# A retention layer and a low-rank mixer on one core: the joint chunk's halves loaded with their own batch, q^T evacuated by two engines, first outputs through two bank pairs, zero matmuls in TensorE's gaps

## The chip, the cores and the metric

The kernel runs on one core of a Trainium2 chip. The metric is the device time of one execution in microseconds (us). The kernel before took 341.96 us as the median of six runs (340.9 to 342.36).

## The reference

q, k and v are (8 batches, 8 heads, 576 positions, 64). The first half is retention: scores times a decay by distance, times v. Its output, with the heads side by side, is x of the second half, a mixer along the sequence with a low rank (32) and a two-layer perceptron.

```python
scores = scale * np.matmul(q, k.transpose(0, 1, 3, 2))
gamma = 1.0 - 2.0 ** (-5.0 - np.arange(H))
Dmat = np.where(rel >= 0, gamma[:, None, None] ** rel[None, :, :], 0.0)
attn = np.matmul(scores * Dmat[None, :, :, :], v)          # (8, 8, 576, 64)
x = attn.transpose(0, 2, 1, 3).reshape(8, 576, 512)
h = x.transpose(0, 2, 1) @ U @ V                           # U (576, 32), V (32, 576)
u = x + h.transpose(0, 2, 1)
out = u + np.maximum(u @ w_ch1, 0.0) @ w_ch2               # (512, 2048), (2048, 512)
```

Inputs and output are float32.

## The kernel before

**Tiling.** Two batches make a pair p: 1152 positions, 9 chunks of 128. Chunks 0 to 3 are of the first batch, 5 to 8 of the second; chunk 4, XC in the code, is the joint chunk: 64 last positions of the first batch (partitions 0 to 63) and 64 first ones of the second (64 to 127). The factor gamma^(m-n) is split: q is scaled by gamma^m (`qscale`), v by gamma^-n (`vscale`), so that a chunk needs only a triangular mask.

**Steps of a chunk.** `load` (L363) issues the loads of k, q, v from SP and the casts to bf16 (ACT, POOL or DVE; the v cast applies the scale, L307). q and k are transposed by TensorE (`t_pe`, L439), in later pairs by a DMA (`t_dma`, L429). `SC` (L502) makes the scores of the chunk with itself in the bank pair `ps_sc` (or, with `apart`, in two of the three banks `ps_big`) and DVE masks them into `ret` (L533). `ST` (L465) adds k^T v to the state S in the bank `ps_s`, and ACT copies it out: `s_sb` (L495), or `sx` (L491) for the last state of the first batch. `RV` (L563) makes ret v plus q S of the chunk before in `ps_o`, and it is copied out as x: in pair 0 as two halves, ACT (L598) and DVE (L600), in later pairs by one DVE instruction (L606). `MA` (L621) makes a = U^T x of a batch, copied out by ACT (`a_sb`, L641). `MH` (L647) adds the mixer's part on DVE, giving u (L670).

**The perceptron** goes over 9 groups of 4 chunks (`mlp`, L731). Y1 is 16 units of 4 matmuls of 128x512 (`uT` by `w1`), each copied out with a relu by ACT (L752). Y2 is 16 units of 4 (4 row tiles by 4 blocks of `w2`), after which DVE adds u (L776) and POOL issues the store (L782). For groups 0 and 1, u^T is built by TensorE (`build`, L689): x^T by matmuls with the identity, plus V^T a, copied out as `uT` (L720, L722).

**The start.** q of batch 0, chunks 0 to 3, comes as one block of 1 MB, four positions beside each other in a partition (`load_q4`, L309); `t_q4` (L329) transposes it and undoes the order while evacuating it (L357 on ACT, L359 on DVE, 512 columns each). Batch 1 has the same with chunks 5 to 8. The loads of pair 0 and of the weights are chained one behind the other in `line` (L957 to 963). The weights come in 16 pieces of 512 KB through six slots, each cast by POOL (L846, L864). POOL also casts V and copies it (`VV`, L816, L824, L826) and U (`UU`, L820).

**The order of the work.** Each step is an Op with an engine, an assumed duration, dependences and a priority, and the planner (`Plan.run`, L52) lists them in the order in which it would run them. The instructions are emitted in that order, so each engine's queue is fixed by the plan, and an instruction that waits holds up all behind it on its engine. Pair 0 is listed by `batch0` (L873) and `batch1` (L899), the others by `front`. Group 0's perceptron is interleaved with batch 1, group g's with batch g+1.

## Time and profile before

| what | value |
|---|---|
| median of six runs | 341.96 us |
| the profiled execution, its own time | 341.8 us |
| its span, first to last instruction | 339.7 us |
| PE busy, mean granted clock | 320.0 us, 0.984 |
| first Y1 matmul of group 0, first Y2 | 30.14, 44.85 us |
| first Y1 matmul of group 1 | 72.68 us |
| last matmul ends | 334.7 us |

All times are from the span's start. PE is TensorE's matmuls, PEld its weight loads, DVE, ACT and POOL are Vector, Scalar and GpSimd engines, SP the one that issues most DMAs (its queue is SPq). A line of the timeline gives start, length, engine, line of the kernel, operation, tiles, shapes and count, and in brackets how long the engine was idle before it and who ended that. A line of the waits gives who waited for whom, the sum in us, how often and the longest. A line of the chain gives start, length and what the work that ended last was doing then. Most matmuls are emitted by one helper (L278), so their tiles tell them apart.

### The profile page before, as it was taken

The page shows a single profiled execution, that of the slowest core. Times are in us where ns is not written, and L with a number is a line of the kernel's source. Part 1 is how long each engine was busy: PE and PEld are TensorE (multiplying, and loading weights), DVE is VectorE, ACT ScalarE, POOL GpSimd, SP SyncE. Part 2 cuts the span into 40 slices and gives each one's busy share as a digit, 9 for nine tenths or more (in the row PEclk, how much of TensorE's full clock was granted, in tenths as well). Part 3 has the DMA queues.
Part 4 walks back from the last instruction along what each step waited for, and adds up shares of the span by engine and source line. Part 5 has one row for each costly group of instructions (what it writes and reads, how often), then busy time and mean ns, then how long its engine had stood idle before and what let it go on. Part 6 is the DMA issues. An engine that isn't in the chain of part 4 may idle for free.

```text
span 339.7 us, 5955 instructions
## 1 busy us (share of the span) xinstructions
PE 320.0 (94%) x2412; PEld 159.1 (47%) x2412; DVE 152.2 (45%) x227; ACT 132.6 (39%) x234; POOL 86.4 (25%) x116
## 2 busy tenths in 40 slices
PE   1689998999999999999999999999999999999993
PEld 0464444556545444554455445445544444444441
DVE  3563128887656646573377429632533020010011
ACT  3455645268601660165214521363135207405600
POOL 5686764142212313131132004200010010010010
PEclk9859999999999999999999999999999999999999
DMA  8999999999999999999999999603110320011011
GB/s 207 203 304 390 385 241 259 203 236 204 230 206 209 229 200 216 214 219 205 199 184 239 204 219 208 158 15 48 62 64 15 71 85 31 0 68 57 0 64 63
DMA packets 153387, 56.19 MB, mean 165 GB/s; under 512 B 144752, under 2 KB 146800, under 8 KB 153360
## 3 DMA queue, kind: packets, MB, share of 16 engines
q1 hardware_dynamic: 150640, 46.90, 68.2%
q0 software_dynamic: 2720, 8.92, 7.8%
q8 instruction: 19, 0.31, 0.4%
q14 instruction: 8, 0.07, 0.1%
HBM read 36.92 MB, written 9.44 MB: 136 GB/s over the span
## 4 chain that ended last, share of the span: by engine, by line
PE 88%; DVE 4%; SPq 3%; POOL 2%; DMA 1%; issue 1%; ACT 1%; POOLq 0%; DVEq 0%
PE ps_big_t L278 73%; PE ps_o L278 6%; PE ps_s L278 5%; PE ps_sc L278 3%; SPq L385 2%; DMA st_st<-in_q_dram 1%; DVE ret_t L533 1%; DVE qkv_t L403 1%; DVE qkv_t L307 1%; PE ps_big_t L452 1%; POOL VV L816 1%; POOL qkv_t L307 1%; DVE o_sb L776 0%; ACT qkT_t L357 0%; DVE x_t L600 0%
## 5 line engine op out<-in xcount | busy, mean ns | idle before, releaser
L278 PE MATMUL ps_big_t<-uT_t,w_sb 128*128 128x512 bf16 x576 | 133.7, 379 | 0.0
L278 PE MATMUL ps_big_t<-w_sb,y_t 128*128 128x512 bf16 x576 | 133.1, 379 | 0.0
L752 ACT ACTIVATE y_t<-ps_big_t 128x512 bf16<-128x512 f32 x144 | 86.0, 597 | 93.7 <-PE ps_big_t L278 93.5
L278 PEld LDWEIGHTS <-w_sb 128*128 128x128 bf16 x576 | 53.9, 98 | 62.4 <-issue 1.9
L278 PEld LDWEIGHTS <-y_t 128*128 128x128 bf16 x576 | 53.8, 98 | 61.5 <-issue 1.1
L776 DVE TENSOR_TENSOR o_sb<-ps_big_t,u_t 128x512 f32<-128x512 f32 x36 | 24.8, 689 | 90.3 <-PE ps_big_t L278 90.3
L782 POOL DMA_DIRECT2D out_dram<-o_sb x34 | 19.4, 570 | 173.1 <-DVE o_sb L776 166.7
L307 POOL TENSOR_TENSOR qkv_t<-st_st,vscale 128x512 bf16<-128x512 f32 x32 | 33.4, 1046 | 55.6 <-DMA st_st<-in_v_dram 44.4
L533 DVE TENSOR_TENSOR ret_t<-ps_sc,tri 128x1024 bf16<-128x1024 f32 x30 | 36.6, 1219 | 19.5 <-PE ps_sc L278 17.8
L495 ACT ACTIVATE s_sb<-ps_s 128x512 bf16<-128x512 f32 x28 | 16.7, 596 | 60.3 <-PE ps_s L278 60.3
L606 DVE TENSOR_TENSOR x_t<-ps_o,qscale 128x512 bf16<-128x512 f32 x27 | 18.6, 689 | 16.8 <-PE ps_o L278 16.7
L670 DVE TENSOR_TENSOR u_t<-ps_s,x_t 128x512 bf16<-128x512 f32 x20 | 13.8, 691 | 22.1 <-PE ps_s L278 22.0
L403 DVE CAST qkv_t<-st_st 128x512 bf16<-128x512 f32 x27 | 19.2, 712 | 4.1 <-DMA st_st<-in_k_dram 4.1
L278 PEld LDWEIGHTS <-qkT_t 64*128 64x128 bf16 (+2 forms) x576 | 14.7, 99 | 13.5 <-issue 7.2
L278 PEld LDWEIGHTS <-ret_t 128*128 128x128 bf16 (+1 forms) x320 | 13.4, 103 | 9.4 <-DVE ret_t L533 1.6
L278 PE MATMUL ps_sc<-qkT_t 64*128 64x128 bf16 (+1 forms) x304 | 13.5, 219 | 4.0 <-ACT qkT_t L459 2.1
L278 PE MATMUL ps_o<-qkv_t,ret_t 128*128 128x64 bf16 (+1 forms) x320 | 15.3, 198 | 0.9 <-DVE x_t L600 0.5
L278 PE MATMUL ps_s<-qkv_t 128*128 128x128 bf16 (+1 forms) x128 | 13.3, 230 | 0.3 <-POOL qkv_t L307 0.3
L459 ACT ACTIVATE qkT_t<-ps_big_t 128x512 bf16<-128x512 bf16 x20 | 11.4, 598 | 3.3 <-PE ps_big_t L452 3.2
L403 DVE CAST qkv_t<-q_st 128x512 bf16<-128x512 f32 x27 | 11.9, 440 | 1.3 <-DMA q_st<-in_q_dram 1.2
L278 PEld LDWEIGHTS <-qkv_t 128*128 128x128 bf16 (+1 forms) x128 | 9.3, 102 | 5.9 <-issue 1.9
L670 DVE TENSOR_TENSOR u_t<-ps_o,x_t 128x512 bf16<-128x512 f32 x16 | 11.0, 685 | 1.7 <-PE ps_o L278 1.5
(75 smaller groups left out, 148.9 us busy)
## 6 DMA issues: line engine op xcount, KB each, us to landing
out_dram<-o_sb POOLq DMA_DIRECT2D x34, 256.0 KB, 3.7
st_st<-in_k_dram SPq DMA_DIRECT2D x32, 256.0 KB, 4.6
st_st<-in_v_dram SPq DMA_DIRECT2D x32, 256.0 KB, 4.8
q_st<-in_q_dram SPq DMA_DIRECT2D x24, 256.0 KB, 5.0
y_t<-in_moe_w_ch_dram SPq DMA_DIRECT2D x10, 512.0 KB, 7.0
wst_t<-in_moe_w_ch_dram SPq DMA_DIRECT2D x6, 512.0 KB, 7.0
q_st<-in_q_dram SPq DMA_DIRECT2D x2, 1024.0 KB, 7.7
st_st<-in_k_dram SPq DMA_DIRECT2D x8, 128.0 KB, 4.6
```

The costliest lines, as they stand in the source:

```text
L278: nc.tensor.matmul(*a, skip_group_check=True, **kw)
L307: eng.tensor_tensor(out=out, in0=f, in1=by[:, :, None].to_broadcast([P, H, D]), op=ALU.mult)
L385: sent.append(nc.sync.dma_start(out=f[rw, :, :], in_=dram[b, :, t0:t0 + rw.stop - rw.start, :].rearrange("h s d -> s h d"),))
L403: nc.vector.tensor_copy(**args)
L459: nc.scalar.activation(out=qkT[slot("qkT", (p, c))][:, j * NHP:(j + 1) * NHP, :], in_=pst(), func=AF.Copy)
L495: nc.scalar.activation(out=s_sb[slot(*sk)], in_=ps_s.rearrange("p (a b) -> p a b", b=P), func=AF.Copy)
L533: nc.vector.tensor_tensor(out=ret[slot(*rk)][:, hl, :, 0:n], in0=bank(hl.start)[:, None] if apart else ps_sc[:, hl, :, 0:n], in1=m[:, None ...
L606: nc.vector.tensor_tensor(out=xs[slot(*xk)].rearrange("p hp hl d -> p hl hp d"), in0=ps_o[:, :, 0:NHP * D].rearrange("p hl (hp d) -> p hl ...
L670: nc.vector.tensor_tensor(out=us[slot(*uk)].rearrange("p (hp hl d) -> p hp hl d", hl=2, d=D), in0=bank().rearrange("p (hp hl d) -> p hp hl ...
L752: nc.scalar.activation(out=y1s[slot(*yk)][:, f, :], in_=ps_big[slot(*bk)], func=AF.Relu)
L776: nc.vector.tensor_tensor(out=osb[slot(*ok)], in0=ps_big[slot(*bk)], in1=us[slot(*uk)], op=ALU.add)
L782: eng.dma_start(out=out_flat[row:row + P, :], in_=osb[slot(*ok)])
```

## The change

The joint chunk of pair 0 is loaded, scaled, transposed and scored in two halves of 64 partitions: the first batch's with batch 0, the second batch's (`b=1`) behind the second q block. V's load moves ahead of k1, U's behind v. q^T is evacuated in eight pieces of 256 columns, ACT and DVE taking one of each chunk's two; one of the four q scalings of batch 0 is fixed on POOL, the other seven on DVE. Outputs x of chunks 1 and 3 go through `ps_sc`, the others through `ps_o`. In pair 0 ACT copies whole outputs, except for the first half of the joint chunk and for chunk 8, which ACT and DVE share. In batch 0 the scores are listed before the states and outputs. `apart` is now for chunks 0, 2 and the joint one. Group 0's Y2 goes through one row tile after the other. The planner runs twice; in the second run it won't start a step of positive priority on ACT or DVE if an urgent one is expected within it. Zero matmuls (`warm`) are put where that plan has gaps of TensorE ahead of the first Y1: 14 of 512 columns in the first, and in the others pieces of 128 columns, one for each 75 ns, as long as a bank is free for them (`ps_s` until the first state, then MA's bank, where they add zero).

```diff
+    zer = sbuf("zer", [P, 512])
...
     def consts_a():
+        nc.vector.memset(zer, 0.0)
...
+    filler = [ps_s]
...
-            st["q", c] = pl.op("DVE", 700.0, ..., [got, ld["consts"]], prio + 0.1, ..., alt=[("POOL", 1050.0)])
+            st["q", c] = pl.op("DVE", 700.0, cast, [got, ld["consts"]], prio + 0.1, acq=[("qkv", (0, c))],
+                               rel=[keys[r]])
+            if r == 3 and par == 0:
+                st["q", c].engs = [("POOL", 1300.0)]
...
-            st["qT", c] = pl.op("ACT", 600.0, ev, pes, prio + 0.1 + i * 0.01, ..., alt=[("DVE", 650.0)])
+            st["qT", c] = [pl.op(e, 400.0, ev, pes, prio + 0.1 + i * step, rel=[sck]) for e in ("ACT", "DVE")]
...
-    def load(p, c, prio, early=False):
+    def load(p, c, prio, early=False, b=None):
+        kb = c if b is None else (c, b)
...
+        pts = parts(p, c) if b is None else parts(p, c)[b:b + 1]
+        rows = slice(0, P) if b is None else pts[0][0]
...
         def fn(e):
+            if first:
+                filler[0] = None
...
-    def RV(p, c, prio, q_done=True):
+    def RV(p, c, prio, q_done=True, b=None, in_sc=False):
...
+        pk = ("sc", ("o", p, c)) if in_sc else ("po", (p, kb))
+        po = ps_sc.rearrange("p a b n -> p a (b n)") if in_sc else ps_o
...
-        if p == 0:
-            st["x", c] = [pl.op("ACT", 390.0, lambda e: half(e, 0), [o], prio, rel=[pk]),
-                          pl.op("DVE", 420.0, lambda e: half(e, 1), [o], prio, rel=[pk])]
+        if p:
+            st["x", kb] = [pl.op("DVE", 700.0, ev, [o], prio, rel=[pk])]
+        elif b == 0 or c == NCH - 1:
+            st["x", kb] = [pl.op(e, 400.0, lambda e, i=i: part(e, slice(i, i + 1)), [o], prio, rel=[pk])
+                           for i, e in enumerate(("ACT", "DVE"))]
         else:
-            st["x", c] = [pl.op("DVE", 700.0, ev, [o], prio, rel=[pk])]
+            st["x", kb] = [pl.op("ACT", 610.0, lambda e: part(e, slice(0, 2)), [o], prio, rel=[pk])]
...
-        if g == 0:
-            seq = [(i, f0) for i0 in (0, 2) for f0 in range(0, NF, 4) for i in (i0, i0 + 1)]
-        else:
-            seq = [(i, f0) for i in range(4) for f0 in range(0, NF, 4)]
-        for i, f0 in seq:
-            pv[i] = Y2(i, f0, pv[i])
+        for i in range(4):
+            for f0 in range(0, NF, 4):
+                pv[i] = Y2(i, f0, pv[i])
...
-    first = [0, 1, 2, 3, XC]
-    line = [ld["q4", 0]] + [ld["k", (0, c)] for c in first] + [ld["q", (0, XC)]]
-    line += [ld["lv"], ld["lu"]] + [ld["v", (0, c)] for c in first] + ld["lw"]
-    line += [ld["q4", 1]] + [ld["k", (0, c)] for c in range(5, NCH)] + [ld["lub"]]
+    XA, XB = (XC, 0), (XC, 1)
+    line = [ld["q4", 0], ld["k", (0, 0)], ld["lv"]] + [ld["k", (0, c)] for c in range(1, 4)]
+    line += [ld["k", (0, XA)], ld["q", (0, XA)]]
+    line += [ld["v", (0, c)] for c in range(4)] + [ld["v", (0, XA)], ld["lu"]] + ld["lw"]
+    line += [ld["q4", 1]] + [ld[x, (0, XB)] for x in "kqv"]
+    line += [ld["k", (0, c)] for c in range(5, NCH)] + [ld["lub"]]
...
+    def warm(n, w):
+        m = P if filler[0] is ps_s else R
+        for _ in range(n):
+            mm(filler[0][0:m, 0:w], zer[:, 0:m], zer[:, 0:w], start=m == P, stop=True)
+
+    pl.run()
+    order = pl.run({o: o.start for o in pl.ops})
+    until = min(o.start for o in pl.ops if o.name == "Y1")
     with tc.manual_schedule():
-        for o, e in pl.run():
+        at = 0.0
+        for o, e in order:
+            if e == "PE" and o.start < until:
+                gap = o.start - at - 150.0
+                if gap > 3000.0:
+                    warm(14, 512)
+                elif gap > 60.0 and filler[0] is not None:
+                    warm(int(gap / 75.0), P)
+                at = o.end
             o.fn(e)
```

## The prediction

> **What bounds the kernel now.** I read the page's slices first, then stretches of a few us, then the waits of PE, then the chain and the timeline of the first 31 us.
>
> ```profile
> span 339.7 us, 5955 instructions
> PE 320.0 (94%) x2412; PEld 159.1 (47%) x2412; DVE 152.2 (45%) x227; ACT 132.6 (39%) x234; POOL 86.4 (25%) x116
> PE   1689998999999999999999999999999999999993
> PEclk9859999999999999999999999999999999999999
> ```
>
> PE is full except in slices 1 to 4, 7, and the last; slice 3 (17.0 to 25.5) has half the clock. From 30 us on PE waits for other engines only four times:
>
> ```profile
> PE ps_sc L278 <- DVE qkT_t L359: 1.5, 1, 1.5
> PE ps_o L278 <- DVE x_t L600: 0.5, 1, 0.5
> PE ps_o L278 <- DVE ret_t L533: 0.3, 1, 0.3
> PE ps_s L278 <- DVE x_t L600: 0.2, 1, 0.2
> ```
>
> That is 2.5 us; asked for 30 to 75 us alone, the waits keep all but the 0.3, and the timeline puts these 2.2 between 54 and 65 us (batch 1). So only two places can give time: the start, up to the first Y1 matmul at 30.14, and batch 1. What comes after has no gap that could close. In the start, by stretches:
>
> ```profile
> 10.00:15.00 5.00, 2.50 (x31) 1.63 (x30) 2.31 (x3) 2.73 (x6) 2.60 (x4) 1.00 1.20 190
> 15.00:20.00 5.00, 3.66 (x54) 3.00 (x54) 4.99 (x9) 2.49 (x5) 4.77 (x8) 0.51 1.30 213
> 20.00:25.00 5.00, 5.00 (x54) 3.45 (x53) 2.61 (x4) 2.26 (x5) 4.56 (x5) 0.50 1.02 354
> 50.00:55.00 5.00, 3.54 (x41) 2.42 (x39) 2.41 (x4) 2.26 (x5) 1.79 (x4) 1.00 1.19 221
> ```
>
> Columns: busy us of PE, PEld, DVE, ACT, POOL, then clock, DMA share, GB/s. From 20 to 25 PE is full, but at half clock: the release comes at 25.3. Until 20 the DMA is full, at some 215 GB/s (256-byte rows of q, k, v). The chain runs through it:
>
> ```profile
> 9.95 4.17 DMA st_st<-in_q_dram
> ...
> 14.25 1.00 POOL qkv_t L307
> 15.25 0.64 POOL VV L824
> ...
> 17.62 1.14 POOL VV L816
> 18.76 0.07 issue
> 18.84 1.05 POOL qkv_t L307
> 19.89 0.04 issue
> 19.93 0.59 PE ps_s L278 x4
> ...
> 28.18 0.61 ACT a_sb L641
> ```
>
> The joint chunk's q, then POOL's preparation of V, then its v casts, then cold PE work up to a_sb. The clock column shows 1.00 until its first record, which misleads: four transposes took 0.61 at 7.33 and 0.38 at 14.52, and the same eight score matmuls 0.40 at 13.54 and 0.61 at 15.35. PE was at half until some 11.7, at full for one stretch of 3.4, at half for 10.2, then at full for good.
>
> **The change part by part.**
> *Fewer bytes ahead of v.* By issue time plus time to landing, v of chunks 0 to 3 land at 16.0, 17.3, 18.5, 19.8, the joint chunk's halves at 20.5 and 21.1. The half chunks of k and q land 0.65 apart. Two of them leave the front (1.3) and U goes behind v (0.5): v3 lands at 18.0, the one v half at 18.6. Three halves and so 1.95 leave the front of the weights, whose last cast ends at 45.15 now and near 43.1 then. The three halves return between the second q block and k5: that block lands at 47.1 - 2.0 = 45.1, but v8 as now (51.5 plus 5 gives 57).
>
> *POOL.* It takes one q scaling instead of two (1.5 each beside DVE; ends 8.1). V (0.66 + 2.54 + 0.66 = 3.9) is cast there now, for V lands second, then k1, k3, the k half (0.61 each; a half has the same free size) and the q half (1.04): with 0.05 between them it reaches v0 at 15.1 and ends v3 at 19.4. Now v3 ends at 22.5 and the joint v on DVE at 23.0. DVE's third q scaling (0.7) ends at 9.4, as the fourth transposes need it now.
>
> *ACT from v0 on.* Whole outputs x0 to x3 go to ACT (0.6 each; now halves of 0.39 on ACT and 0.42 on DVE). In a row: s0, x0, s1, x1, s2, x2 (six of 0.6), sx 0.77, x3 0.6, half of the joint output 0.39, at 0.05 to 0.1 between them. From 16.5 this ends at 22.4; ST3 (19.9) waits for s2, and sx for it. The joint term of MA and the queued builds take 0.6: a_sb starts at 23.0, where it is 28.18 now. From a_sb to Y1 took 1.96: Y1 at 25.0, 5.2 earlier. q^T goes in eight evictions of 256 columns on two engines. No row shows them; the nearest are the x halves, 0.39 on ACT and 0.42 on DVE, and a whole one of 512 takes 0.60 and 0.69, so a half costs at least 0.30. Four in a row take 1.2 to 1.7 (I take 1.6) instead of the 2.7 from 10.32 to 13.0 now; either way they end before 12, under POOL's queue. ps_sc as second output bank removes waits like the 0.5 above; without it ACT would still be the longer chain. Both at 0.
>
> *Zero matmuls.* 14 of 512 columns, from about 1.2 on. At full clock 16 of that size took 3.65, and the last unit of 4 took 1.03, so 0.22 each; at half clock 0.43 (a single one shows the same difference, 0.61 against 0.39): 6.0 in all, done before the q block's scaling (7.3), so free. The memset in DVE's queue ahead of lngt costs some 0.3, under DVE's wait for POOL of 1.14. The small ones fill three quarters of the planned gaps; a gap shorter than planned is overrun by at most 9 x 0.056 = 0.5 (one transpose took 0.23, seven 0.56), and that before v0 has come, while PE has nothing else that is due: 0. Once v0 is there the bank ps_s is in use and there are none.
> The Trainium skill (TensorE: Matmul & The Clock Gate, part 1) says full clock comes after one busy window of 3.4 us and goes after an idle one. The row is harsher: from 18 to 22 PE was busy 3.7 of 4 us and stayed at half, and from 11.7 to 15.1 it was busy some 1.2 of 3.4, not idle, and lost the clock. By the page's rule the change needs only the 14, and the sum holds; by the row it also needs the fill between 8 and 16. Beside this stands 50 to 55, with 3.54 of 5 at clock 1.00: some 70% holds a clock that is there. From 16 on there are no fillers, but PE's own work there (0.22 + 0.4 + 0.3 + builds and MA, over 1.0 per 1.3) is above that. I take full clock.
>
> *Weights as a floor.* Y2 starts at 25.0 + 14.7 (30.14 to 44.85 now) - 0.4 (the joint ST goes) = 39.3. The order of Y2 goes to row tile by row tile, so the fourth weight block is wanted after three units of 0.87, its second half at 42.3, but cast at 43.1: 0.8 of PE lost. Ends: 0, if Y1 starts later by that; 1.5, if the weights gain only 1.3.
>
> *Batch 1.* Seven Y2 units are done at 46.2, and the q block lands at 45.1. Now PE takes 22.65 from its first transposes (50.03) to Y1 of group 1 (72.68), 2.2 of it waiting. One Y2 unit less (0.87) and one joint ST more (0.39): 20.0 of work, so 66.2 without waits. DVE has 4 x 0.7 + 0.7 + 4 x 0.4 + 0.69 + 4 x 1.22 + 4 x 0.69 for adds + 0.7 + 0.4 + 1.4 and casts of 3: some 19 us from 45.1, just enough. Stepping through the order, the score rounds (PE 0.4, mask 1.22, and the Y2 units between them) put SC8 at 60.7, RV8 at 63, a_sb at 64.7. Waits of 0.7 to 2.5, I take 1.2: Y1 of group 1 at 67.4, 5.3 earlier. v8 at 57 is in time. POOL's third store waits for an add behind DVE's second mask (54.8), and stands ahead of the casts of v6 and v7; with 0.6 for it v6 is ready at 56.5 and v7 at 57.5, two to three us before ST6 and ST7 are due (58.5, 60.7).
>
> *Afterwards.* The order of group 1 is nearly the present one. Batch 2's loads land as now (k, q of chunk 2: 68.3; chunk 3: 72.8; joint: 77.4) and are transposed now at 77.9, 82.4 and 86.4: 9 us spare, of which 5.3 is used. So the gain stays. 341.8 (the profiled execution: span 339.7 and 2.1 around it) - 5.3 = 336.5; the median of the runs is 0.16 higher: 336.7.
>
> **Rivals.** *The clock is not held* (against it: the 70% stretch; for it: 18 to 22). Then S0 to a_sb takes 9.9 as now, or 12 if no release comes by the end; from 16.3 that gives 26.2 to 28.2 for a_sb, a gain of 0 to 2: 340.5.
> *The gain is given back in batch 1.* Y2 is its filler and is 5 us further on, but v8 lands as now. Waits of 4 instead of 1.2 in PE's order: 339.4. For it: DVE is full from 55 to 60 already; against it: ACT takes over four outputs.
> *Slower.* PE's order puts the four score rounds, which share ps_sc, behind DVE's queue (out adds, v casts) between Y2 units that cannot move. If each round slips by 1.4 (a 0.69 add and a v cast that contends, as the one of 2.43 at 56.3, ahead of the mask), 5.6 is lost and it ends at 342.1; it decides from 1.3 per round.
> *It doesn't do what it says*: the fillers run after the data came, and delay it; they would take 6.0 from 7: this needs zer late, and DVE has nothing ahead of it.
>
> **How the numbers follow.** Forecast 0.66, its own range 334.8 to 338.2 (POOL and weight terms of +-1, waits +-1). Clock 0.10, given back 0.15, slower 0.09. About 0.3% (1.0 us) is what a measurement of this kernel can tell from no change: faster takes the forecast, the given-back case and 0.06 of the clock case, 0.87; same 0.04; slower 0.09. Range 334.5 to 340.3: it leaves the slower case and the bottom of the forecast out.
>
> **What would show it.** Clock 1.00 in every stretch from 10 on (a first record of 0.5 there would make the clock case); POOL's fourth v cast ending near 19.4; a_sb near 23.0; Y1 near 25.0; one PE wait for a w_sb cast near 42 to 43; Y1 of group 1 near 67.4, with 1 to 2 us of waits for DVE in 46 to 66; from then on no waits and the same 267 us to the end. Y1 at 25 and Y1 of group 1 above 70 is the given-back case. It would be wrong if v0 waited for POOL beyond 17, or if ACT's row broke up.

## The result and the profile after

The changed kernel takes 342.98 us (median of 18 runs, 341.43 to 344.22), the kernel before 341.55 in the same comparison (339.96 to 343.09): the ratio is 1.0043, interval [1.003, 1.0055]. It is slower by some 0.4%, where a gain, to 336.7, had been forecast. Its profiled execution took 339.9, with a span of 337.7. That is 3 us below the kernel's own median, so there are two things to explain: why this trace is not at 336.5, and why most executions are longer than it.

The page of the changed kernel, its first lines and two rows of the slices:

```profile
span 337.7 us, 6077 instructions
PE 325.6 (96%) x2470; PEld 160.2 (47%) x2470; DVE 149.6 (44%) x230; ACT 134.3 (40%) x239; POOL 87.0 (26%) x118
PE   7879989999999999999999999999999999999994
PEclk9999999999999999999999999999999999999999
```

The zero matmuls fill most of slices 1 and 2 (counted from 1, 8.4 us each), no slice has less than full clock, and slice 6, at 42 to 51 us, has an 8 that was a 9 before. The waits of PE from 30 us on:

```profile
PE ps_sc L367 <- DVE qkv_t L347: 1.5, 2, 1.3
PE ps_s L302 <- DVE x_t L662: 0.2, 1, 0.2
```

Three of the four waits of before are gone; the one of 0.2 is still there. A new one stands at 48 us: the transposes of the second q block wait for DVE's scaling of it. The stretches, columns as before (busy us of PE, PEld, DVE, ACT, POOL, then clock, DMA share, GB/s):

```profile
10.00:15.00 5.00, 4.21 (x74) 3.30 (x71) 3.64 (x8) 3.20 (x9) 4.85 (x8) 1.00 1.37 198
15.00:20.00 5.00, 4.19 (x82) 3.01 (x79) 4.21 (x7) 3.29 (x7) 3.99 (x5) 1.00 0.97 167
20.00:25.00 5.00, 3.91 (x54) 2.47 (x54) 1.06 (x2) 2.25 (x6) 2.91 (x4) 1.00 0.95 324
45.00:50.00 5.00, 3.70 (x23) 1.68 (x21) 2.72 (x5) 0.63 (x1) 1.08 (x3) 1.00 1.23 209
```

The kernel before, 45 to 50:

```profile
45.00:50.00 5.00, 5.00 (x25) 2.25 (x23) 2.14 (x2) 1.86 (x3) 2.95 (x3) 1.00 1.00 203
```

PE at full clock is ahead of its data: from 20 to 25 it was full at half clock, now it idles 1.1 of 5 us. And 45 to 50, where PE was full, now has 1.3 us idle. The chain of this stretch (changed kernel):

```profile
27.54 8.25 DMA y_t<-in_moe_w_ch_dram
35.80 0.05 issue
35.85 1.05 POOL w_sb L922
36.90 0.02 issue
36.92 0.37 SPq L915
37.29 0.05 issue
37.34 10.61 DMA q_st<-in_q_dram
47.95 0.02 issue
47.97 0.04 DVE qkv_t L347
```

It runs through weights (load, POOL's cast that frees the slot, SP's next issue) and then 10.6 us through the second q block, not through the work of the start. The marks of the traces, in us:

| | first Y1 | first Y2 | scaling of q block 2 starts | Y1 of group 1 | span |
|---|---|---|---|---|---|
| before | 30.14 | 44.85 | 47.15 | 72.68 | 339.7 |
| forecast of the steps | 25.0 | 39.3 | 45.1 | 67.4 | 334.4 |
| after | 26.78 | 41.06 | 47.97 | 71.14 | 337.7 |
| after, three more executions | 27.04, 26.51, 27.04 | 41.31, 40.78, 41.32 | 48.04, 48.23, 48.88 | 71.18, 71.37, 71.76 | 338.7, 340.6, 338.8 |

Of 3.4 us that the start gains, 1.5 are left at the Y1 of group 1. The rest of the head start is waited away in between.

### The profile page after: what moved, and what is told of

It is laid out like the page before. It is cut to its first block, busy times and chain, and to the rows that moved or that the text cites. A ratio compares the mean times of both kernels' runs of the same rounds, so it can differ in the third digit from the quotient of the medians.

```text
span 337.7 us, 6077 instructions
## 1 busy us (share of the span) xinstructions
PE 325.6 (96%) x2470; PEld 160.2 (47%) x2470; DVE 149.6 (44%) x230; ACT 134.3 (40%) x239; POOL 87.0 (26%) x118
## 4 chain that ended last, share of the span: by engine, by line
PE 82%; DMA 8%; SPq 5%; DVE 2%; issue 1%; POOL 1%; ACT 0%; DVEq 0%
PE ps_big_t L302 69%; PE ps_s L302 5%; DMA y_t<-in_moe_w_ch_dram 5%; PE ps_o L302 4%; SPq L412 4%; PE ps_sc L302 3%; DMA q_st<-in_q_dram 3%; PE ps_big_t L492 1%; DVE qkv_t L347 1%; SPq L862 0%; SPq L895 0%; SPq L870 0%; DVE qkv_t L430 0%; POOL w_sb L922 0%; POOL w_sb L904 0%
## 5 line engine op out<-in xcount | busy, mean ns | idle before, releaser
L302 PEld LDWEIGHTS <-y_t 128*128 128x128 bf16 x576 | 53.7, 98 | 61.1 <-issue 0.8
L843 POOL DMA_DIRECT2D out_dram<-o_sb x34 | 19.4, 570 | 166.5 <-DVE o_sb L837 153.5
L434 POOL TENSOR_TENSOR qkv_t<-st_st,vscale 128x512 bf16<-128x512 f32 x34 | 35.5, 1046 | 59.9 <-DMA st_st<-in_v_dram 44.5
L730 DVE TENSOR_TENSOR u_t<-ps_s,x_t 128x512 bf16<-128x512 f32 x20 | 13.8, 690 | 23.2 <-PE ps_s L302 23.1
L430 DVE CAST qkv_t<-q_st 128x512 bf16<-128x512 f32 x27 | 16.1, 597 | 1.8 <-DMA q_st<-in_q_dram 1.8
L302 PE MATMUL ps_o<-qkv_t,ret_t 128*128 128x64 bf16 (+1 forms) x304 | 14.1, 193 | 0.0
L501 ACT ACTIVATE qkT_t<-ps_big_t 128x512 bf16<-128x512 bf16 (+1 forms) x21 | 11.4, 558 | 6.3 <-PE ps_big_t L492 6.2
L430 DVE CAST qkv_t<-st_st 128x512 bf16<-128x512 f32 x27 | 13.2, 487 | 1.3 <-DMA st_st<-in_k_dram 1.2
L302 PE MATMUL ps_s<-qkv_t 128*128 128x128 bf16 (+1 forms) x128 | 12.5, 219 | 0.5 <-ACT s_sb L543 0.5
L302 PEld LDWEIGHTS <-qkv_t 128*128 128x128 bf16 (+1 forms) x128 | 8.6, 97 | 5.9 <-issue 1.5
```

Source lines behind the costliest of these rows:

```text
L302: nc.tensor.matmul(*a, skip_group_check=True, **kw)
L430: nc.vector.tensor_copy(**args)
L434: eng.tensor_tensor(out=qkv[slot(*qk)][rows, 2, :, :], in0=at(2)[rows], in1=vscale[rows, c, :, None].to_broadcast([rows.stop - rows.start, ...
L501: nc.scalar.activation(func=AF.Copy, **args)
L730: nc.vector.tensor_tensor(out=us[slot(*uk)].rearrange("p (hp hl d) -> p hp hl d", hl=2, d=D), in0=bank().rearrange("p (hp hl d) -> p hp hl ...
L843: eng.dma_start(out=out_flat[row:row + P, :], in_=osb[slot(*ok)])
```

## The experiments

Each was compared with the kernel before on its own chip (some share one). Where not said otherwise, a version is an edit of the changed kernel.

**The kernel unedited, and its parts.** First once more, then with U's load ahead of v, then without zero matmuls, then with Y2 of group 0 by pairs of row tiles.

> The changed kernel once more, unedited, for a second trace: the first profiled execution (339.9) lies 3 us below the median of the changed kernel's other executions (342.98). Theory A (the gain of the start is given back in batch 1, because the second q block lands at 48.0, no earlier than before): the trace looks like the first one, Y1 of group 0 near 26.8, second q block near 48, and the missing 3 us show as a still later q block or later v casts, PE waiting for DVE in 46 to 66. Theory B (the clock): in a typical execution PE loses full clock for one or more stretches of 3.4 us, in the start or after the wait near 48, and the time is lost there. Ratio to before 1.003 to 1.006.

Measured: 343.1, ratio 1.0027 [1.0003, 1.0051]; the profiled execution took 340.85, with full clock again and 2 us below the median again, so neither expected loss is in it.

```diff
+    line += [ld["k", (0, XA)], ld["q", (0, XA)], ld["lu"]]
+    line += [ld["v", (0, c)] for c in range(4)] + [ld["v", (0, XA)]] + ld["lw"]
```

> U's two loads ahead of v, as in the kernel before; all else as changed. Theory A says that the weights are issued at 17.6, as before, because the second U load holds SP for 1.6 us right ahead of them: here the first weight piece is issued near 16.5, the last weight cast ends 1 us earlier (44.1), the second q block lands near 47, PE does not wait 1.1 for UU, and the time falls by 1 to 1.5 us against the changed kernel. The rival, that the six slots and POOL's casts set the pace of the weights whatever the issue, has the last cast end at 45.1 and the time within 0.5 us.

Measured: 342.35, 1.0009 [0.9982, 1.0036], undecided. U is in time, but now PE waits 1.3 us for POOL's fourth v cast, from 19.0 on, and in the trace the clock goes to half right behind that hole, from 21.9 to 32.2. The first Y1 is at 30.57 and the Y1 of group 1 at 74.03.

```diff
-                if gap > 3000.0:
-                    warm(14, 512)
-                elif gap > 60.0 and filler[0] is not None:
-                    warm(int(gap / 75.0), P)
```

> The changed kernel without any zero matmul. If the data of batch 1 bound the kernel (A), the start runs at half clock again, Y1 of group 0 comes 1 to 3 us later, but the wait at 48 shrinks by as much: time within 0.7 us of the changed kernel. If the fillers are what gains (or the clock is what decides, B), it is 2 us or more slower. If the fillers are what costs in the typical execution, it is faster.

Measured: 341.15, 0.9987 [0.9962, 1.0013]: 2 us better than the changed kernel on the same chip. The clock is released at 22.4 for the first time and then stays; the first Y1 is only 1 us later (27.75), and the Y1 of group 1 is at 71.54. So the zero matmuls bring nothing that lasts, and cost some 2 us in the median.

```diff
+        if g == 0:
+            seq = [(i, f0) for i0 in (0, 2) for f0 in range(0, NF, 4) for i in (i0, i0 + 1)]
```

> The changed kernel with group 0's Y2 in the order of before (two row tiles in turn per weight block). No wait for a weight cast shows in the first trace (28 matmuls in 6.4 us), so by A the time stays within 0.7 us. If the order of Y2 is what fails to cover batch 1's waits in the typical execution, it is 1 us or more faster.

Measured: 345.14, 1.01 [1.0067, 1.0133]: slower. Two-microsecond stretches of its trace:

```profile
50.00:52.00 2.00, 0.91 (x12) 0.71 (x12) 1.94 (x4) 1.47 (x4) 0.39 (x2) 1.00 1.10 218
52.00:54.00 2.00, 0.91 (x12) 0.64 (x10) 1.97 (x5) 1.43 (x5) 0.47 (x2) 1.00 0.57 108
54.00:56.00 2.00, 1.36 (x17) 0.96 (x17) 0.85 (x2) 1.72 (x5) 1.98 (x5) 0.70 1.17 248
56.00:58.00 2.00, 1.78 (x11) 0.65 (x10) 0.00 (x0) 1.05 (x2) 2.00 (x2) 0.50 1.19 297
```

Two stretches with PE under half busy, then half clock for 3.4 us (54.8 to 58.2) in dense work. The shortest stretch between two changes of the clock is 3.41 us in the traces here, and the others are multiples of it; it is called a window below. The Y1 of group 1 comes at 74.46.

**Zero matmuls alone.** The kernel before, with nothing but the zero matmuls in its own plan's gaps.

> The kernel before with the zero matmuls alone (14 of 512 columns and the small ones in its own plan's gaps). Theory B (an early release only opens the way to a drop of the clock in a dense stretch, where it costs; without fillers PE is cold while it waits anyway, and is released once for good): the time is 0.5 to 2 us above that of before, with mean clocks below 0.995 in most executions. Rival, the one of the forecast: PE at full clock from 16 to 25 saves 2 to 4 us of the start, of which batch 1 gives back some: 1 to 2 us faster.

Measured: 340.97, 0.9986 [0.9965, 1.0008]. Neither a cost nor a gain shows in the kernel before, so both expectations missed. The first Y1 is at 27.91 in its trace, 2.2 earlier than before, and the Y1 of group 1 at 72.39, 0.3 earlier. Here too the second q block (scaling from 48.20) takes the gain. Seven of the nine executions have a mean clock of 0.990 to 0.995; in the trace the one window at half is at 14.4 to 17.9, ahead of the dense work.

**Is it the data of batch 1?** k and v of chunks 5 to 8 read as contiguous rows of 2 KB in place of eight pieces of 256 bytes (they hold other positions), without zero matmuls.

> The changed kernel without zero matmuls, and with k and v of batch 1's chunks 5 to 8 read as contiguous 2 KB rows in place of 256-byte rows: the same bytes and instructions, but other positions of k and v come to stand in these chunks, so that part of the result is another one. Theory A (the data of batch 1 bound the stage from 47 to 71): k8 and v8 land 2 to 4 us earlier, Y1 of group 1 comes 1.5 us or more earlier than the 71.5 of the kernel without fillers, and the time falls by 1 to 2.5 us. Rival (DVE's and PE's own order bound it): within 0.6 us.

Measured: 341.02, 0.9983 [0.997, 0.9996], beside 341.15 and 0.9987 with the normal loads (another chip). The k and v behind the q block are not what batch 1 waits for: from the block's scaling (47.30) to the Y1 of group 1 (70.56) it takes 23.26, as with the normal loads (23.28).

**The q block ahead of the last weights**, with Y2 by pairs and no zero matmuls:

```diff
+    line += [ld["v", (0, c)] for c in range(4)] + [ld["v", (0, XA)], ld["lu"]] + ld["lw"][:12]
+    line += [ld["q4", 1]] + ld["lw"][12:] + [ld[x, (0, XB)] for x in "kqv"]
```

> The changed kernel without zero matmuls, with the second q block loaded ahead of the last four weight pieces, and group 0's Y2 in the order of before, since the last weight pieces then come later. A says the wait for the second q block near 48 goes (it lands near 43): 0.5 to 1.5 us faster than without the move, if the later k and v of batch 1 don't become the next bound; the rival within A that k5 to v8 are what bounds gives no change.

Measured: 341.79, 1.0014 [0.9998, 1.0029]. The block is there at 40.99, 7 us earlier, but the Y1 of group 1 comes at 75.23. PE's waits from 30 to 80:

```profile
PE ps_s L302 <- POOL qkv_t L434: 2.5, 1, 2.5
PE ps_sc L367 <- DVE qkv_t L347: 0.6, 1, 0.6
```

What POOL waited for then was the load of v:

```profile
59.57 1.04 POOL L434 TENSOR_TENSOR qkv_t<-st_st,vscale 128x512 bf16<-128x512 f32 x1 [4.58 <-DMA st_st<-in_v_dram]
```

v's arrival takes the block's place, and one window at half clock (61.6 to 65.0) follows. The block's arrival stops being the limit, and the next one is no better.

**Without zero matmuls, and U ahead of v** (the two edits above together), run twice on two chips:

> The changed kernel without zero matmuls and with U ahead of v. If U's place costs what the first trace shows (1.1 us of PE's wait for UU, weights issued 1 us late), and no clock is lost, it is 0.3 to 1 us faster than without the zero matmuls alone; if batch 1's data bound, only what the weights gain arrives, and 0.5 us at most.

> The version without zero matmuls and with U ahead of v, unedited, a second time: 340.3 and a ratio of 0.9975 to the kernel before, if the first result holds. Its spread (338.3 to 343.1 the first time) is put down to the moment of the release, which no zero matmul prepares: a trace with a first Y1 near 27 has it before 23 us, one near 30 has it behind 28.

Measured: 340.28, 0.9975 [0.9957, 0.9993], and 340.44, 0.9965 [0.9946, 0.9984]. It is faster than the kernel before by 0.3%, and so than the changed kernel too. The expected cause did not show: the weights are issued a microsecond earlier than in the changed kernel (16.55 and 16.30 instead of 17.61), but their last cast starts at 43.46 and 43.12, where it started at 43.42 without the move of U. The q block did not come earlier either (49.09, 48.30; without the move 48.26). In the second trace the clock is released at 22.9 and the first Y1 is at 27.87, as expected.

**The joint halves behind the k**, on top of that version:

```diff
+    line += [ld["q4", 1]] + [ld["k", (0, c)] for c in range(5, NCH)] + [ld["lub"]]
+    line += [ld[x, (0, XB)] for x in "kqv"]
```

> This is the version without zero matmuls and with U ahead of v, in which the three loads of the joint chunk's second half (64 rows, two transfers of each) no longer follow the second q block but stand behind the k of chunks 5 to 8 and the second U. A (the transfers queued right behind the q block take a share of the DMA engines and so delay it; the stretch from its landing to the first Y1 matmul of group 1 is fixed at some 23.2 us): the block lands near its 9.7 us after issue as in the kernel before instead of 10.6 to 11, 1 us earlier than in the version with the halves in place (49.1, so about 48), and the first Y1 matmul of group 1 follows 23.2 later: 71.3 instead of 72.4; time about 339.3. B (the block is held by its slots' and the weights' pace, and the next loads, now k, share the engines just as the halves did): landing and Y1 within 0.3 of 49.1 and 72.4; time 340.3. C (the joint halves then come too late for their transposes): the block earlier, but Y1 of group 1 not; PE waits for a joint q or k cast between 55 and 68.

Measured: 344.23, 1.0039 [1.0013, 1.0065]: slower. The block is earlier (it lands at 45.97, and DVE starts on it at 47.38 without waiting), so the halves do delay it, as A says; but the Y1 of group 1 is at 72.52, 25.1 later instead of 23.2. That is C by the marks, but not by its cause: for a cast of q or k PE waits 0.2 us. The units of Y2, which cover waits, are through at 61.1 in this order (64.3 in the second run without the edit), and from 62 to 67 DVE is full and PE idles 0.95 (0 there):

```profile
62.00:67.00 5.00, 4.05 (x63) 2.43 (x63) 5.00 (x7) 3.43 (x6) 1.91 (x3) 1.00 0.95 225
```

In its trace there is a second loss, much later. DVE and PE from 148 on, and the stretches:

```profile
148.21 0.43 DVE L430 CAST qkv_t<-st_st 128x512 bf16<-128x512 f32 x1 [3.12 <-DMA st_st<-in_k_dram]
148.55 0.68 DVE L648 TENSOR_TENSOR x_t<-ps_o,qscale 128x512 bf16<-128x512 f32 x1
...
149.29 0.29 PE L302 MATMUL ps_o<-s_sb,qkT_t 64*128 64x64 bf16 x8 [2.41 <-DVE x_t L648]
```

```profile
146.00:148.00 2.00, 0.88 (x11) 0.33 (x10) 0.00 (x0) 0.97 (x2) 0.82 (x1) 1.00 1.17 231
148.00:150.00 2.00, 0.71 (x10) 0.38 (x10) 1.67 (x4) 0.00 (x0) 0.76 (x2) 0.87 1.20 224
150.00:152.00 2.00, 2.00 (x6) 0.67 (x5) 0.92 (x1) 0.56 (x1) 1.03 (x1) 0.50 1.20 291
```

A k of a later batch landed late, DVE waited 3.1 us for it with an output x queued behind the cast, PE waited 2.4 us for that, and the hole cost one window of half clock as well (149.5 to 152.9). Ten of the 22 executions have a mean clock of 0.993 to 0.995 (this one 0.995), and average 346.2; the eleven at 0.996 and more average 342.5. By an estimate a window at half costs at most half of its length, 1.7 us, so these 3.7 us are not the clock alone: a low mean clock also marks executions in which late data made a hole.

**Only the 14 large zero matmuls, and a look at the changed kernel's clock.**

> The changed kernel with the 14 zero matmuls of 512 columns ahead of the q block kept, and the small ones in the planned gaps left out. A (the early release is what costs: full clock is granted near 5 to 7 us, the sparse stretch from 8 to 16 then takes it away, or a later dense stretch loses it): some executions have a mean granted clock below 0.995, and the median lies between the version without any (341.15) and the changed kernel (343.0): about 342. B (the small ones alone cause the later drops, by the steady load that they put on PE): no drops, 341.1, the same as the version without any. C (the 14 alone cause them): 343, as the changed kernel.

Measured: 343.13, 1.0029 [1.0014, 1.0043], every execution with a mean clock of 0.985 or less: C by the time, but not as a late drop. The trace (345.11) has full clock from 3.9 to 10.7, loses it behind a stretch with PE 0.40 of 2 us busy (6 to 8), and is at half until 21.0. Its first Y1 is nevertheless at 27.11, close to the changed kernel's; what is late is the second q block (scaling from 49.98) and with it the Y1 of group 1 (74.39). So a time above the changed kernel's median can come about with no loss of clock behind 21 us.

> The changed kernel once more, unedited, for one more profiled execution. Both profiled ones so far (339.9 and 340.85) are 2 to 3 us below the median of its runs (343.0), and their clock column never falls. If the theory holds that the missing 2 us are a later loss of clock, an execution near 343 shows one to three windows of 3.4 us at half clock behind 20 us, and every mark ahead of the drop (Y1 near 27.0, the second q block near 48.0) as in the other two. If it is something else, the marks ahead differ with the clock full throughout. An execution near 340 again leaves this as it is.

Measured: 342.79, no drop of the clock worth a window. Up to the Y1 of group 1 (71.37) it is like the others; behind it this waits, which the 339.9 has nowhere:

```profile
PE ps_o L302 <- DVE ret_t L583: 1.8, 4, 0.8
```

So there is a second way to be slow: waits for DVE in later batches. Late loads in its queue, as in the trace above, were the guess to test.

**Cheap loads for batches 2 to 7**, beside the changed kernel unedited:

> The changed kernel unedited, beside the next three on one chip: 343 (340 to 344.5), ratio to the kernel before about 1.003. Its trace: Y1 near 27, Y1 of group 1 near 71.3, and behind it 0 to 2 us of waits of PE for DVE.

Measured: 342.15, 1.0006 [0.9976, 1.0036]: in these nine runs no difference from the kernel before shows. PE has no waits for other engines behind 72 in the trace (340.94).

```diff
+                    if p and len(pts) == 1:
...
+                            out=f.rearrange("p h d -> p (h d)"),
+                            in_=dram[bb].rearrange("h s d -> (h s d)")[m:m + P * H * D].rearrange("(p x) -> p x", p=P),
```

> The changed kernel, with q, k and v of the full chunks of batches 2 to 7 read as contiguous rows of 2 KB in place of eight pieces of 256 bytes (so they hold other positions; sizes, casts, stores and their order stay). A (loads of batches 2 to 7 pace the rest): no waits of PE for DVE behind 72, the DMA share falls well below 1 from 75 to 220, every execution ends like the lucky ones, median 340 and a narrow spread. B (the clock, lost again after an early release, is what costs): nothing changes in the first 70 us, some executions keep a mean clock of 0.98 to 0.99 and the median stays at 342.5 to 343. C (both): 341 to 342, the ones with a clock above 0.997 near 339.5.

> The same cheap loads of batches 2 to 7 in the changed kernel without its zero matmuls. A and C: 339.5 and narrow, as no drop of the clock and no late load is left; the Y1 of group 1 near 71.5 plus 266.6 plus 2.1. B: 341, as the version without zero matmuls had (341.15), since its clock did not drop there and its loads were no cost.

> The kernel before with the same cheap loads of batches 2 to 7: its PE waits 0.3 us behind 72, so at most 0.3 us is to be had if loads are in time there. A: within 0.5 us of the kernel before (341.5), its spread a little narrower. If it gains as much as the changed kernel does (2 us or more), the loads' lateness is not what takes the changed kernel's head start, but a cost that both have.

Measured: 342.9, 1.0042 [1.0025, 1.006]; without zero matmuls 342.05, 1.0027 [1.001, 1.0043]; the kernel before with them 343.0, 1.0049 [1.0032, 1.0067]. A is refuted as an explanation of the medians: with the DMA share down from some 1.1 to 0.8 (75 to 120), nothing gets faster, and the kernel before gets slower (its PE then waits 1.8 us for DVE behind 72, where it waited 0.3). The zero matmuls make 0.85 us in this pair, which is not clear of noise. Both traces of the changed start show the clock at work. With zero matmuls:

```profile
18.00:20.00 2.00, 1.78 (x41) 1.37 (x40) 0.87 (x4) 1.81 (x5) 1.01 (x2) 1.00 0.47 75
20.00:22.00 2.00, 0.70 (x3) 0.27 (x4) 1.06 (x1) 0.43 (x1) 1.24 (x2) 0.79 0.99 289
22.00:24.00 2.00, 2.00 (x25) 1.19 (x23) 0.00 (x0) 1.35 (x3) 1.08 (x2) 0.50 0.99 322
```

PE waits 1.4 us for POOL's UU, is busy 0.70 of 2, and the clock is at half from 21.2 to 31.4: the first Y1 is at 30.89, and the Y1 of group 1 at 73.81, 2.0 to 2.7 later than in the four traces of the changed kernel. The start of this version has the changed kernel's instructions. Without zero matmuls nothing releases it before 31.7:

```profile
28.44 1.04 PE L302 MATMUL ps_big_t<-VV,a_sb 128*128 128x512 bf16 x2 [0.69 <-ACT a_sb L708]
29.27 1.06 PE L302 MATMUL ps_sc<-VV,a_sb 128*128 128x512 bf16 x2
30.12 0.63 PE L302 MATMUL ps_s<-a_sb,VV 128*128 128x512 bf16 x1
30.55 0.63 PE L302 MATMUL ps_o<-a_sb,VV 128*128 128x512 bf16 x1
30.98 3.97 PE L302 MATMUL ps_big_t<-uT_t,w_sb 128*128 128x512 bf16 x16
```

The pairs take 1.04 and 1.06 here and 0.60 at full clock. The same start, released at 22.4, had its first Y1 at 27.75; here it is at 30.98. The mean clock of this execution is given as 1.0: it counts no half clock ahead of the first release, so for versions without zero matmuls it says nothing of the start.

**Filling the one hole.** 16 zero matmuls ahead of the first UU matmul, and, in the version with U ahead of v, ahead of the fourth chunk's state matmuls. The latter go into the state's bank and wipe what chunks 0 to 2 of pair 0 had added there for heads 0 and 1, so that version leaves this part of the result out.

```diff
+            if split and ts[0][1] == 0:
+                for _ in range(16):
+                    mm(bank()[0:R, 0:P], zer[:, 0:R], zer[:, 0:P], start=True, stop=True)
```

> The changed kernel, with 16 more zero matmuls of 128 columns (0.056 us each at full clock, 0.9 in all) ahead of the first UU matmul, into the bank that it is going to write. PE waits there 1.1 us for UU in the changed kernel, so they cost nothing while the clock is full. A (the hole near 20.6 lets the clock go in part of the executions, which costs two to four us at the first Y1): hardly an execution has a mean clock below 0.993, the first Y1 is at 27 in the trace, and the median is near 341, 1.5 to 2 below the changed kernel's 343; its spread shrinks to that of the version without zero matmuls or less. B (the clock is lost elsewhere: at 6 to 10, 24 or 48 to 52 us): as many low clocks as before and a median of 342.3 to 343. C (they delay the UU matmul): Y1 later than 27.3 in a trace with full clock.

> The version with U ahead of v and zero matmuls, which waits 1.3 us for the fourth v instead of UU, with 16 zero matmuls ahead of the fourth chunk's state matmuls. A: median 340.3 to 341 (the same version without them had 342.35, and 340.56 in its executions without a low clock). B: 342.3 again. C: the state matmuls of the fourth chunk start later than 20.3.

Measured: 343.5, 1.007 [1.0046, 1.0093], and 341.27, 1.0001 [0.9986, 1.0015]. The hole is filled (PE busy 1.74 of 2 from 20 to 22, first Y1 at 27.05), and the executions with the lowest clock go: in the first none of 8 is below 0.987, in the second none of 22 below 0.989, where the changed kernel has 14 of 43 at 0.985 or less. But others at 0.987 to 0.992 stay (4 of the 8, at 343.1 to 345.3): B. The first gains nothing (the changed kernel had 342.15 on this chip). The second lies between A and B, 1.1 below its counterpart, but on another chip, and the ratios (1.0001 and 1.0009) are not clear of each other. Without zero matmuls that version had 340.44 on the same chip, 0.8 less, with intervals of the ratio that don't overlap. The hole at 20.6 is one of several places, and its filling does not bring the time back.

## Why the prediction was wrong

**Table of the clock.** All runs of the changed kernel (43), grouped by the mean clock that their own records give; one window of 3.4 us at half lowers it by 0.005:

```
mean clock          executions   mean us
0.996 and more          13       341.27
0.993 to 0.995           9       342.65
0.988 to 0.992           6       343.10
below 0.988             15       343.13
kernel before, 0.996 and more   185   341.55
kernel before, below 0.988       33   341.92
```

**The sum.** The median is 6.3 us above the forecast. 3.4 of them are in the profiled execution already (339.9 for 336.5), in two terms: the second q block and the stretch behind it. Some 1.7 go with a lower clock, by the table. The rest is that the profiled execution was itself 1.4 below the mean of those with full clock, which is luck as far as the runs tell.

**The weights and the second q block: wrong, and the largest step.** The prediction said that three halves leave the front, so that all weights and with them the second q block come 1.95 earlier, at 45.1. The block came at 47.97, 0.8 later than before. SP's issues of the start, changed kernel and version without zero matmuls:

```profile
15.95 1.61 SPq L862 DMA_DIRECT2D ust<-in_moe_U_dram  x1
17.61 1.10 SPq L895 DMA_DIRECT2D wst_t<-in_moe_w_ch_dram  x2
```

```profile
16.42 0.52 SPq L862 DMA_DIRECT2D ust<-in_moe_U_dram  x1
16.98 1.10 SPq L895 DMA_DIRECT2D wst_t<-in_moe_w_ch_dram  x2
```

The first weights are issued at 17.61 (17.64 before), since the same issue of U takes 1.61 us instead of 0.52, and the DMA runs dry meanwhile (46 GB/s from 18 to 19; share 0.59 from 18 to 20, 1.26 before). Of all that is queued ahead of the weights the last lands at 19.76, 1.3 earlier than before (21.05), and 1.2 of that is lost until the last weights have landed. By an estimate from the shares that is this hole: 0.59 from 18 to 20 and 0.88 from 20 to 22 are 1.2 us short of a full DMA. From 26 to 44 nothing makes it up: the DMA is full there in both kernels, with a share of 1.03 to 1.07 and 367 to 394 GB/s, a piece of 512 KB lands every 1.36 us, and POOL, whose casts take 1.04, waits for it. So POOL and the slots keep up, and the DMA sets the pace. The last cast of the changed kernel:

```profile
44.03 1.04 POOL L922 CAST w_sb<-y_t 128x1024 bf16<-128x1024 f32 x1 [0.34 <-DMA y_t<-in_moe_w_ch_dram]
```

It ends at 45.08; 45.15 before, 43.1 in the forecast. So of the 1.95 only 0.07 arrived.

The held issue goes with something that the DMA view counts as "instruction": one packet of 16 KB.

```profile
q8 instruction: 1, 0.02, 5.5%
```

(changed kernel, 15.7 to 17.2.) In 16 of the 20 traces the first such packet starts between 15.6 and 18.9 us, and in each of them one issue of SP, for v, U or the weights, takes 0.7 to 1.5 us longer than usual and ends 0.4 to 0.9 us behind the packet. The other four have it at 20.5 to 23.2, and no such issue there. The zero matmuls move it: all eleven traces with them have it at 15.6 to 17.8, the nine without them at 17.9 or later, five of these with a held issue too, such as this one (no zero matmuls; usual are 0.47):

```profile
18.12 1.88 SPq L895 DMA_DIRECT2D y_t<-in_moe_w_ch_dram  x1
```

I had counted SP's queue as untouched by the zero matmuls. What the packet loads, and why SP is held, no run shows. In the two traces of the changed start without a held issue (U ahead of v and no zero matmuls, second run; halves behind the k) the last cast ends at 44.16 and 43.99, 1.0 and 1.2 earlier than before.

And behind the block stand the three halves that were moved back there. It lands 10.61 us after its issue (9.65 before), and 3.97 behind the last weights (3.08). The traces agree: 3.0 to 3.1 in all four without the halves behind the block (the version with the halves behind the k is one), 3.9 to 5.8 in the 15 with them (the version with the block ahead of the last weights is left out). With the halves behind the k that delay goes, and is paid for elsewhere.

**Batch 1: mechanism right, sum nearly right.** From the block's scaling to the Y1 of group 1 I had 22.3 us (45.1 to 67.4), measured were 23.2, and 22.9 to 23.4 in twelve more of the traces above; 25.5 before. So the Y1 of group 1 is 3.74 late: 2.87 from the block, 0.87 from the stretch behind it. "Y1 at 25 and Y1 of group 1 above 70 is the given-back case", the prediction said; this is what happened in the profiled execution (339.9, where that rival had 339.4). The cause it named, v8 and 4 us of waits for DVE, is not the one. v8 did land late, at 60.98 instead of the forecast 57 (56.26 before; the 51.5 plus 5 of the prediction make 56.5), but PE waits for no v; its waits from 30 us on sum to 1.7, 1.5 of them for the block's scaling. With cheap k and v the block came 1.0 earlier than with the normal ones (47.30, 48.26) and the Y1 of group 1 by the same 1.0, the stretch between them unchanged. But no run shows what a much earlier block alone would bring: in the two that moved it in the queue another wait or order took its place.

**The start: right in direction, two terms short.** a_sb was to come at 23.0 and came at 24.83. v3 lands at 18.99 instead of 18.0, so POOL ends its cast at 20.1, not 19.4. And PE waits 1.1 us for UU, a wait that I had not named: with U behind v, POOL casts U right behind the fourth v, from 20.05 on. Why v3 is late is not shown; it was issued at 12.89, ahead of the held issue. From a_sb to Y1 it takes 1.95, as taken. One reading was off, without weight for the result: slice 4 of the row of before is a 9, so the slices in which PE was not full are 1 to 3, 7 and the last.

**"I take full clock": wrong for two executions in three.** It holds in the profiled execution. But 30 of 43 have a lower clock, and they are 1.7 us longer in the mean (342.98 against 341.27; 1.1 to 2.4 within each of the three comparisons). The zero matmuls release the clock at 4 to 7 us; PE, then twice as fast, outruns its data and idles at 6 to 10, at 20.6 and at 48 us. In traces of its variants such holes took the clock away again, for one window or three. That they do so in its own longer executions is concluded from the table, not seen, and the table alone does not part the cost of the clock from that of the late data that make the hole. The group with one window is 1.4 longer, within the 1.7 that half a window makes. For three windows from 21 us on the traces show it: first Y1 at 30.57 and 30.89 instead of 26.5 to 27.0. The kernel before has the same three windows at half in 33 of its 220 runs, and they cost it 0.4: in its trace they fall at 15.1 to 25.4, and the start up to 11.7 is cold as well.

I had weighed the row against the rule of the Trainium skill (TensorE: Matmul & The Clock Gate, part 1), full clock after one busy window and half only after an idle one, and taken its side. The rows are harsher both ways. Changes of the clock lie a multiple of 3.41 us apart within a trace, so the traces can be cut into such windows. Two that ended in half clock (with cheap loads and zero matmuls; with the halves behind the k):

```profile
17.75:21.16 3.41, 2.03 (x44) 1.48 (x42) 2.18 (x4) 2.49 (x5) 2.42 (x3) 1.00 0.68 141
146.09:149.50 3.41, 1.00 (x19) 0.45 (x16) 1.17 (x3) 0.89 (x2) 1.57 (x2) 1.00 1.16 224
```

PE was busy in 60 and 29% of them, not idle. Over the 20 traces at full clock, all five windows with PE busy 28 to 48% lost it, of 23 with 50 to 60% three did, and none above did. (A few matmul records can be missing, so the shares are rough.) The changed kernel's own traces have windows of 52 to 60% busy that kept it: it runs near the edge, which goes with a clock that falls in some executions and not in others. And in the trace with the late release PE was busy from 18 to 27 us with under 0.3 missing, more than two windows, and stayed at half.

The page calls the number of cold matmuls "run-variable", by where the window lies. That the release varies the runs confirm, but three executions with the same start, released at 20.9, 22.4 and 31.7, differ by more than one window. Its estimate that the cold ramp is below 1% of a span is not contradicted (1.7 of 338 is 0.5%), only that here 1% was all there was to win.

**Afterwards.** From the Y1 of group 1 to the span's end it takes 266.6 in the profiled execution and 267.0 before, as said.

**What stays open.** Executions of the changed kernel with full clock average 341.27, 0.3 below the kernel before, though its profiled ones with full clock are 0.9 to 1.5 earlier at the Y1 of group 1. The difference of 0.3 is not clear of noise, but some 1 us is missing, in later batches. One trace shows 1.8 us of it as waits for DVE, but cheap loads did not bring it back, so it is not settled. Nor is it known where each loss of the clock falls in the longer executions: the traces show it at 10.7, 14.4, 21.2, 21.9, 54.8, 61.6 and 149.5 in other versions, and in none of the changed kernel's own. And the zero matmuls cost 2 us in the changed kernel (0.85 with cheap loads, not clear of noise) and nothing that was found in the kernel before; why is open. The clock is not all of it: with U ahead of v and the hole filled, the 13 executions at full clock average 341.4, and 340.4 is the mean of the version without zero matmuls on the same chip.

## What to carry to other kernels

Before counting a gain at the start, find the first transfer behind it whose arrival is paced by something that the change does not touch, here weights that fill the DMA from 26 to 44 us and a q block behind them; the head start ends there. Loads moved from ahead of such a transfer to right behind it are not out of its way: they still share the DMA with it. Zero matmuls that release the clock are of use only if real work keeps PE busy from then on: an engine that is fast before its data come makes holes, and in several traces here a hole took the clock back at a time when it costs more. And compare executions by their own clock before trusting one trace: the profiled one here was the fourth fastest of 43.

## What was not expected of the hardware

The clock is lost behind windows of 3.41 us in which PE is still 28 to 60% busy, for one or three such windows, and in the same program in some executions and not in others. Without zero matmuls it was released at 20.9 and 22.4 us in two traces and at 31.7 in a third whose start has the same instructions. An issue of SP's queue takes 0.7 to 1.5 us longer in each of the 16 traces in which a 16 KB "instruction" packet starts between 15.6 and 18.9 us; zero matmuls on PE, which wait for nothing and touch no DMA, come with an earlier packet (15.6 to 17.8). A q block of 1 MB lands 3.0 to 3.1 us behind the last weights with k loads queued behind it, and 3.9 to 5.8 with half chunks there. Loads with eight times longer rows, in batches 2 to 7, made the kernel before slower, 1.0049 [1.0032, 1.0067].
